# One hand-written instruction order for blocks 1 to 6 of the feed-forward half of an FNet layer

## The chip, the cores and the metric

The kernel runs on one core of a Trainium2 chip. Its engines are TensorE (PE, with its weight loads shown apart as PEld), VectorE (DVE), ScalarE (ACT), GpSimd (POOL) and SyncE (SP). The metric is device time in microseconds for one launch. Lower is better.

## The reference

The input x has 2048 rows of 576 values. It is normalised row by row, and three things are added: x itself, a Fourier mixing of the normalised rows, and a two-layer perceptron of them with 4608 hidden units.

```python
xn = layernorm(A_x)
a = xn @ dft_hid_re.T;  b = xn @ dft_hid_im.T
fourier = dft_seq_re @ a - dft_seq_im @ b          # 2048x2048 times 2048x576, twice
mlp = maximum(xn @ B_w1, 0) @ B_w2                 # 576 -> 4608 -> 576
out = A_x + fourier + mlp
```

## The kernel before

All products run in float16 as three partial products (high times high, high times low, low times high). So each operand is first scaled by a power of two and split: ACT writes the high half, DVE the remainder. Large products are done by seven block products in place of eight (Strassen's scheme), which adds sums and differences of operands on DVE.

The perceptron is cut into nine blocks of 512 hidden units (`b` = 0 to 8) and, inside each, four groups of 512 rows (`g` = 0 to 3). One `(b, g)` is a step, numbered t = 4b + g. A step has two pairs of hidden tiles (`i` = 0, 1). Each pair takes seven block products P1 to P7 of seven matmuls each (L495, function `product`), which gather in PSUM banks. What frees the banks is: a copy of P1, P6 and P5 on ACT (L521, L523, L524), and an addition of P2, P7 and P3 on DVE (L522, L525, L526). Then come the rectified values, split by ACT (L502) and DVE (L503), four sums on DVE (L506 to L509), and their split (L514 on ACT, L517 on DVE). The second layer of a step runs one step later: seven block products of twelve matmuls each (L566, `products2`; block 0 has four plain ones instead, L615), each followed by its eviction (L579 on ACT or L581 on DVE, `blocks2`). A finished sum is added to a buffer in DRAM by a DMA that POOL issues (L588, `add2`).

Beside this, each block prepares the weights of the next:

- SP loads two halves of w1, five DMAs each (L164, then L175 and L176 twice), and two of w2 (L152). All four halves share two buffers, `raw_w`.
- DVE takes the largest absolute value of each w1 half in two reductions (L652, `max_w1`). POOL finds it over the partitions (L202), and DVE makes the scale of it (L205 to L210, `power`). For w2, ACT sums absolute values (L718, `sum_w2`) and the same `power` follows.
- ACT and DVE split the weights (L676, L681, L682; L771, L775), and DVE forms the sums for Strassen's scheme (L698 to L701, L751 to L754).

Three more streams run along: SP loads tiles of the Fourier matrices (L1049, `first_c`), and ACT sums their absolute values (L1056, `sum_c`); there is one buffer for these tiles, so a load waits for the sum before it. In blocks 2 to 5 POOL issues one DMA in each step that adds a part of x to the DRAM buffer (L640, `add_x`).

Order is set in two ways. Between `begin()` and `end_hand()` every engine runs its instructions in the order in which the program writes them. Outside, a scheduler chooses each engine's order by its own estimates; `after(i)` holds an instruction behind another one there. Before the change, the hand order covers block 0 (a list of words, `ORDER`) and the first step of block 1, t = 4. The scheduler orders t = 5 to t = 35, where the loop over `steps` writes a step's products and takes pieces of weight preparation from the list `todo` at fixed points.

Of the kernel before, what the change touches and what calls it, by code (L numbers as in the profile page):

```python
# [18 lines left out]
P = 128  # L19
S = 2048  # L20
# [30 lines left out]
ORDER = """  # L51
# [24 lines left out]
tw:3:3 tu:3:2 od:3:3 tv:3:2:G rw:1 tw:3:2 rm:0  # L76
"""
# [3 lines left out]
def kernel(  # L81
# [394 lines left out]
    def pair_products(b, g, i):  # L476
# [5 lines left out]
        h = hs[b, g, i] = mlp.tile([P, 2, 7, GH], F16, tag="h", name=f"h{b}_{g}_{i}", bufs=4)  # L482
        st = mlp.tile([P, 5, GH], F32, tag="stage", name=f"s{b}_{g}_{i}")
        r21, s1, s2, s3, s4 = (st[:, n] for n in range(5))
        u, v, w = (banks1[k][0] for k in (i, 2, 3))
        c11, c22 = cbufs[i], cbufs[2]
        tt, stt = nc.vector.tensor_tensor, nc.vector.scalar_tensor_tensor

# [11 lines left out]
        def value(q, src):  # L500
            hi, lo = h[:, 0, q], h[:, 1, q]
            nc.scalar.activation(hi, src, AF.Relu)  # L502
            stt(lo, src, 0.0, hi, ALU.max, ALU.subtract)  # L503

        def end_s():
            stt(s3, c11, 0.0, r21, ALU.max, ALU.subtract)  # L506
            stt(s1, c22, 0.0, r21, ALU.max, ALU.add)
            stt(s2, c22, 0.0, s3, ALU.max, ALU.subtract)
            stt(s4, u, 0.0, s2, ALU.max, ALU.subtract)  # L509

        hi_s, lo_s = (h[:, k, S1 : S4 + 1] for k in range(2))

        def end_hi():
            order["s"] = nc.scalar.activation(hi_s, st[:, 1:], AF.Copy).ins  # L514

        def end_lo():
            order["lo"] = nc.vector.tensor_tensor(lo_s, st[:, 1:], hi_s, ALU.subtract).ins  # L517


        free = {  # L520
            P1: lambda: freed(nc.scalar.activation(c11, u, AF.Copy)),  # L521
            P2: lambda: freed(tt(c11, v, c11, ALU.add), "vfree"),  # L522
            P6: lambda: freed(nc.scalar.activation(s1, u, AF.Copy)),  # L523
            P5: lambda: freed(nc.scalar.activation(c22, w, AF.Copy)),  # L524
            P7: lambda: freed(tt(c22, u, c22, ALU.add), "vfree"),  # L525
            P3: lambda: freed(tt(r21, w, s1, ALU.add), "vfree"),  # L526
        }
        use = {
            P2: lambda: value(A11, c11),
            P7: lambda: value(A22, c22),  # L530
            P3: lambda: nc.scalar.activation(r21, r21, AF.Relu),
            P4: lambda: (value(A12, u), end_s(), ends.extend((end_hi, end_lo))),
        }

        def run(n, used=False):
            if used:
                return use[n]()
            product(n)
            if n in free:
                free[n]()  # L540
# [3 lines left out]
    places, sums = {}, {(r, j): None for r in range(2) for j in range(2)}  # L544
# [11 lines left out]
    def products2(b, g, n):  # L556

        qa, qb, first, row, col = PRODUCTS[n]
        if first:
            places[n] = ps2.tile([P, 2, 512], F32, tag="ps2", name=f"p2_{b}_{g}_{n}")[:, :, :EH]  # L560
        ps = places[PLACE[n]]
# [10 lines left out]
    def blocks2(b, g, n):  # L572

        row, col = PRODUCTS[n][3:]
        ps = places[PLACE[n]]
        o = sums[row, col]
        if n in (0, 2, 3, 6):
            o = sums[row, col] = sumbufs[sum_buffer(g, n)]
            freed(nc.scalar.activation(o, ps, AF.Copy, scale=us[b]))  # L579
# [4 lines left out]
    def add2(g, n):  # L584

        row, col = PRODUCTS[n][3:]
        if n not in (0, 2, 3):
            nc.gpsimd.dma_start(spill[g, row, col], sums[row, col], accum_op=ALU.add)  # L588
# [16 lines left out]
    def plain2(g, k):  # L605

        row, col = BLOCKS0[k]
        ps = places[0, k] = ps2.tile([P, 2, 512], F32, tag="ps2", name=f"p2_0_{g}_{k}")[:, :, :EH]
# [12 lines left out]
    def block2(g, k, eng=nc.scalar):  # L621

        o = sums[BLOCKS0[k]] = sumbufs[(4 * g + k) % 3]
        ps = places[0, k]
# [81 lines left out]
    def sum_w2(b, i):  # L706
# [3 lines left out]
        if b:  # L710
# [71 lines left out]
    def split_w2(b, i, c):  # L782
        if b and c == 0:
# [23 lines left out]
    def prepare_w2(b):  # L807
# [5 lines left out]
        if b == 1:  # L813
            p = steps1.pop(3)
# [676 lines left out]
```

## Time and profile before

| | |
|---|---|
| median of 3 runs | 1284.52 us (1283.21 to 1284.97) |
| the profiled execution, its own time | 1281.2 us |
| its span, first to last instruction | 1279.4 us |
| mean granted TensorE clock | 0.996 |
| PE busy in the span | 1222.7 us (96%) |
| DVE busy | 1019.5 us (80%) |
| ACT busy | 754.3 us (59%) |
| POOL busy | 213.9 us (17%) |
| DMA traffic | 175.97 MB, 138 GB/s on average |

Step t = 4 begins at 110.66 us in the span, block 2 at 204.11, block 7 at 638.94. Perceptron work ends near 812, and the two Fourier stages fill the rest. In the rows below, L-numbers are lines of the kernel before. `p` is a PSUM tile of the second layer, `bank` one of the first layer, `accs`, `dbuf` and `wbuf` are large SBUF buffers that hold several things. Where a row says "idle before", the engine sat idle ahead of that instruction, and the name behind the arrow is what ended the wait.

### The profile page before, as it was taken

How to read it: one execution, taken by the hardware profiler on the slowest of the kernel's cores; microseconds unless marked ns; L12 is line 12 of the kernel's file. 1: busy time of each engine (PE TensorE's matmuls, PEld its weight loads, DVE VectorE, ACT ScalarE, POOL GpSimd, SP SyncE). 2: the span in 40 equal slices, each digit the busy share in tenths (PEclk: the TensorE clock that was granted, in tenths of full speed). 3: DMA queues.
4: the chain of work that ended last, by engine and by line, in shares of the span. 5: the costliest groups of instructions: out<-in, count | busy, mean ns of one | idle time of the engine just before them, and what ended most of it. 6: DMA issues, size and time to landing. Idle time of an engine off the chain costs nothing.

```text
span 1279.4 us, 26160 instructions
## 1 busy us (share of the span) xinstructions
PE 1222.7 (96%) x10394; PEld 993.2 (78%) x10394; DVE 1019.5 (80%) x1968; ACT 754.3 (59%) x1334; POOL 213.9 (17%) x279
## 2 busy tenths in 40 slices
PE   6999999999998999999999999799999999999998
PEld 6856778788887887888888888576777777777777
DVE  7875887888877878988789878869877757888785
ACT  7664667667666676766776756645544445543332
POOL 2641111222132212111211111100111110000000
PEclk9999999999999999999999999989999999999999
DMA  7996565886778658666575777511755541155440
GB/s 225 201 190 163 130 133 117 172 170 114 166 147 168 130 121 177 141 142 145 122 156 119 161 168 162 135 36 66 199 116 144 116 101 24 59 190 161 154 127 33
DMA packets 127051, 175.97 MB, mean 138 GB/s; under 512 B 48336, under 2 KB 88784, under 8 KB 126928
## 3 DMA queue, kind: packets, MB, share of 16 engines
q1 hardware_dynamic: 98256, 122.38, 32.3%
q0 software_dynamic: 28672, 51.92, 27.4%
q8 instruction: 81, 1.33, 0.4%
q14 instruction: 42, 0.34, 0.1%
HBM read 112.53 MB, written 56.62 MB: 132 GB/s over the span
## 4 chain that ended last, share of the span: by engine, by line
PE 53%; DVE 19%; issue 12%; DMA 6%; ACT 5%; POOL 3%; SPq 1%; POOLq 0%; DVEq 0%; ACTq 0%
PE p L1358 20%; PE p L566 13%; PE bank L495 13%; PE pd L1211 6%; DMA raw_w<-in_w_dram 2%; POOL spill L588 2%; DVE h L517 1%; DVE cs L775 1%; DVE h L503 1%; DVE R L1171 1%; DVE w2s L775 1%; DMA accs<-in_x_dram 1%; DMA accs<-in_cim_dram 1%; DMA raw_d<-in_dft_dram 1%; ACT f L1056 1%
## 5 line engine op out<-in xcount | busy, mean ns | idle before, releaser
L566 PE MATMUL p<-w2s,h 128*128 128x288 f16 x2688 | 367.7, 286 | 9.8 <-ACT sums L579 2.5
L1358 PE MATMUL p<-R,cs 128*128 128x288 f16 x2688 | 333.4, 287 | 5.7 <-DVE accs L1368 3.4
L1358 PEld LDWEIGHTS <-cs 128*128 128x128 f16 x2688 | 263.3, 98 | 75.5 <-issue 5.1
L566 PEld LDWEIGHTS <-h 128*128 128x128 f16 x2688 | 262.2, 98 | 74.7 <-issue 10.1
L495 PEld LDWEIGHTS <-wbuf 128*128 128x128 f16 x1568 | 153.3, 98 | 31.5 <-issue 10.5
L495 PEld LDWEIGHTS <-dbuf 128*128 128x128 f16 x1568 | 153.1, 98 | 29.8 <-issue 8.6
L771 ACT ACTIVATE cs<-tb,sc_c 128x1024 f16<-128x1024 f32 x56 | 63.8, 1147 | 86.1 <-PE p L1358 50.6
L495 PE MATMUL bank<-xT,dbuf 128*128 128x256 f16 x896 | 111.6, 273 | 0.0
L495 PE MATMUL bank<-xT,wbuf 128*128 128x256 f16 x896 | 111.1, 273 | 0.3 <-ACT accs L524 0.3
L502 ACT ACTIVATE h<-accs 128x256 f16<-128x256 f32 x128 | 51.9, 412 | 90.3 <-DVE accs L525 67.5
L517 DVE TENSOR_TENSOR h<-s,h 128x1024 f16<-128x1024 f32 x64 | 78.0, 1219 | 22.9 <-ACT h L514 22.5
L588 POOL DMA_DIRECT2D spill<-dbuf x70 | 63.3, 923 | 190.7 <-DVE dbuf L581 165.4
L495 PE MATMUL bank<-accs,wbuf 128*128 128x256 f16 x672 | 86.4, 272 | 7.8 <-DVE accs L525 5.2
L775 DVE SCALAR_TENSOR_TENSOR cs<-tb,sc_c,cs 128x1024 f16<-128x1024 f32 x56 | 71.5, 1281 | 27.5 <-ACT cs L771 27.1
L495 PE MATMUL bank<-accs,dbuf 128*128 128x256 f16 x672 | 86.7, 272 | 6.0 <-DVE accs L525 3.4
L514 ACT ACTIVATE h<-s 128x1024 f16<-128x1024 f32 x64 | 67.5, 1055 | 25.5 <-DVE s L509 25.1
L771 ACT ACTIVATE cs<-accs,sc_c 128x1024 f16<-128x1024 f32 x39 | 44.2, 1145 | 56.8 <-PE p L1358 25.6
L588 POOL DMA_DIRECT2D spill<-wbuf x42 | 38.2, 910 | 190.7 <-DVE wbuf L581 172.7
L1056 ACT ACTIVATE f<-f 128x1024 f32<-128x1024 f32 x64 | 66.9, 1046 | 1.0 <-DMA f<-in_cim_dram 0.9
L503 DVE SCALAR_TENSOR_TENSOR h<-accs,h 128x256 f16<-128x256 f32 x128 | 52.8, 417 | 15.9 <-ACT h L502 15.3
L775 DVE SCALAR_TENSOR_TENSOR cs<-accs,sc_c,cs 128x1024 f16<-128x1024 f32 x39 | 50.0, 1281 | 16.2 <-ACT cs L771 15.8
L1178 ACT ACTIVATE R<-tb 128x288 f16<-128x288 f32 (+1 forms) x64 | 39.3, 621 | 37.8 <-DVE tb L1202 29.0
(226 smaller groups left out, 1877.1 us busy)
## 6 DMA issues: line engine op xcount, KB each, us to landing
spill<-dbuf POOLq DMA_DIRECT2D x80, 288.0 KB, 4.7
f<-in_cre_dram SPq DMA_DIRECT2D x32, 512.0 KB, 5.7
f<-in_cim_dram SPq DMA_DIRECT2D x32, 512.0 KB, 5.7
spill<-wbuf POOLq DMA_DIRECT2D x48, 288.0 KB, 5.0
raw_w<-in_w_dram SPq DMA_DIRECT2D x18, 576.0 KB, 4.4
raw_w<-in_w_dram SPq DMA_DIRECT2D x17, 512.0 KB, 6.7
accs<-in_cim_dram SPq DMA_DIRECT2D x16, 512.0 KB, 4.8
tb<-in_cre_dram SPq DMA_DIRECT2D x16, 512.0 KB, 4.8
```

The costliest lines, as they stand in the source:

```text
L495: nc.tensor.matmul(ps, l, r, start=first and m == 0, stop=m == len(todo) - 1, skip_group_check=not first,)
L502: nc.scalar.activation(hi, src, AF.Relu)
L503: stt(lo, src, 0.0, hi, ALU.max, ALU.subtract)
L514: order["s"] = nc.scalar.activation(hi_s, st[:, 1:], AF.Copy).ins
L517: order["lo"] = nc.vector.tensor_tensor(lo_s, st[:, 1:], hi_s, ALU.subtract).ins
L566: nc.tensor.matmul(ps[:, c], h[:, x, qa, c * P : (c + 1) * P], w[:, y, qb], start=first and i == 0 and j == 0, stop=i == NQ - 1 and j == 2 ...
L588: nc.gpsimd.dma_start(spill[g, row, col], sums[row, col], accum_op=ALU.add)
L771: nc.scalar.activation(hi, src, AF.Copy, scale=s)
L775: nc.vector.scalar_tensor_tensor(lo, src, s, hi, ALU.mult, ALU.subtract)
L1056: nc.scalar.activation(f, f, AF.Abs, scale=2.0**-10, accum_out=sums_c[:, n, q : q + 1])
L1211: nc.tensor.matmul(ps, x[:, k, c * P : (c + 1) * P], dsp[z][:, a, y], start=first and m == 0, stop=m == len(PASSES) - 1, skip_group_check= ...
L1358: nc.tensor.matmul(ps, w[:, a, RANK[k]], r[:, c, RIGHT[rq]], start=first and k == 0 and j == 0, stop=k == HK - 1 and j == 2, skip_group_ch ...
```

## The change

The hand order is extended to t = 27, the last step of block 6. `ORDER` becomes `BLOCK0`, unchanged, and three lists follow: `BLOCK1` (blocks 1 and 2), `BLOCK` (one block, run four times, for blocks 3 to 6) and `FLUSH` (three words left over). A word names one small piece of work and where it belongs: `p:0:1:5` is product P5 of pair 1 in the block's step 0; `f:` frees its bank (a trailing A or V names ACT or DVE); `h:` and `l:` are the split of rectified values, `r:`, `x:`, `y:`, `H:`, `L:` the rest of a pair's work. `m:-1:4` is the second layer's block product number 4 of the step before, `e:` its eviction, `a:` its addition in DRAM, `X:` the addition of x. `F:` and `S:` are `first_c` and `sum_c`. For the next block's weights, `L1:` and `L2:` load w1 and w2, `mx:` is a w1 reduction, `sw:` the sum of w2, `R:` starts `power` on POOL and `ph:` ends it on DVE, `nh:`, `nl:`, `uh:`, `ul:` are the splits and `ns:`, `us:` the sums. The scheduler now orders t = 28 to t = 35 alone.

```diff
-ORDER = """
+BLOCK0 = """
+BLOCK = """
+p:0:0:1 e:-1:0:A F:1:0 a:-2:6 p:0:0:5 ul:0:0:2 f:0:0:1:A X:1 m:-1:1 ul:0:1:1 f:0:0:5:A L1:1:0
+p:0:0:6 e:-1:1 S:1:0 m:-1:2 a:-1:1 f:0:0:6:A p:0:0:2 L1:1:1 e:-1:2:V m:-1:3 f:0:0:2 h:0:0:11
+l:0:0:11 m:-1:4 e:-1:3:V m:-1:5 F:1:1 e:-1:4 mx:1:0 a:-1:4 m:-1:6 e:-1:5 mx:1:1 a:-1:5 p:0:0:3
+e:-1:6:A R:1:0 p:0:0:7 f:0:0:3 a:-1:6 ph:1:0 r:0:0 p:0:1:5 f:0:0:7 nh:1:0:0 mx:1:2 p:0:1:1
...
+        def copy_of(dst, src, eng):
+            if eng is nc.scalar:
+                freed(nc.scalar.activation(dst, src, AF.Copy))
+            else:
+                freed(nc.vector.tensor_copy(dst, src), "vfree")
...
+        def free(n, eng=nc.scalar):
+            if n in (P1, P5):
+                copy_of(*{P1: (c11, u), P5: (c22, w)}[n], eng)
+            elif n == P6:
+                copy_of(stage_of(1), u, eng)
...
-    def blocks2(b, g, n):
+    def blocks2(b, g, n, eng=nc.scalar):
...
+            if eng is nc.scalar:
+                freed(nc.scalar.activation(o, ps, AF.Copy, scale=us[b]))
+            else:
+                freed(nc.vector.tensor_scalar(o, ps, us[b], None, ALU.mult), "vfree")
...
-    for n in range(4, len(steps)):
+    def run_block(words, b, stop):
+        for word in words.split():
+            name, at, *args = word.split(":")
+            at = int(at) + (b if name in by_block else b * NG)
+            key = (name, at, *(a for a in args if a not in ENG))
+            late = at > stop // NG if name in by_block else at >= stop - (name in "mea")
+            late = late or key in held
+            if key in done or late or name == "X" and not 2 * NG <= at < 6 * NG:
+                continue
+            done.add(key)
...
+    LAST = 7 * NG
+    held = {(c, LAST - 1, "1") for c in "HLS"}
+    run_block(BLOCK1, 1, LAST)
+    for b in range(3, NB - 2):
+        run_block(BLOCK, b, LAST)
+    run_block(FLUSH, NB - 3, LAST)
+    ends += [pair(LAST - 1, 1)["H"], pair(LAST - 1, 1)["L"]]
+    end_hand()
+    passes = passes[2 * (LAST - NG) :]
+    for n in range(LAST, len(steps)):
...
-        if n == NG:
-            end_hand()
```

The instructions are the same but for 24 evictions that move from ACT to DVE (12 copies of 256 columns, 12 scalings of 576); and the values that `sum_w2` throws away go to the w2 tile in place of a staging tile. Three places show what the lists do to the order.

First DVE, at the head of block 3, around the two reductions of the first w1 half of block 4 (`raw_w1_4_0`). `h3_1_0` is a value of block 3, group 1, pair 0; `p2_3_0_1` is the second layer's product 1 of block 3, group 0. Before:

```order
L581 SCALAR_TENSOR_TENSOR wbuf_97<-p2_3_0_1_4307,c_ub_4050,wbuf_97 128x576
L525 TENSOR_TENSOR accs_98<-bank0_1754,accs_98 128x256
L503 SCALAR_TENSOR_TENSOR h3_1_0_4240<-accs_98,h3_1_0_4240 128x256
L522 TENSOR_TENSOR accs_98<-bank2_1756,accs_98 128x256
L526 TENSOR_TENSOR s3_1_0_4241<-bank3_1757,s3_1_0_4241 128x256
L652 TENSOR_REDUCE c_mf_4414<-raw_w1_4_0_4295 128x1
L503 SCALAR_TENSOR_TENSOR h3_1_0_4240<-bank0_1754,h3_1_0_4240 128x256
L506 SCALAR_TENSOR_TENSOR s3_1_0_4241<-accs_98,s3_1_0_4241 128x256
```

And with the change (L805 is `max_w1` there, L732 and L734 are evictions in `blocks2`, L632 and L628 free banks):

```order
L628 TENSOR_TENSOR accs_98<-bank2_1756,accs_98 128x256
L619 SCALAR_TENSOR_TENSOR h3_0_0_4105<-accs_98,h3_0_0_4105 128x256
L732 TENSOR_SCALAR wbuf_97<-p2_2_3_3_4091,c_ub_2821 128x576
L734 SCALAR_TENSOR_TENSOR wbuf_97<-p2_2_3_0_3995,c_ub_2821,wbuf_97 128x576
L805 TENSOR_REDUCE c_mf_4139<-raw_w1_4_0_4047 128x1
L734 SCALAR_TENSOR_TENSOR dbuf_96<-p2_2_3_3_4091,c_ub_2821,dbuf_96 128x576
L805 TENSOR_REDUCE c_mf_4139<-raw_w1_4_0_4047 128x1
L814 TENSOR_REDUCE c_mw1_4136<-c_mf_4139 128x1
L632 TENSOR_TENSOR s3_0_0_4075<-bank3_1757,s3_0_0_4075 128x256
```

The reductions moved from the work of block 3's group 1 to that of its group 0, a step earlier, with one eviction between them and the freeing of a bank (L632) behind.

Second SP, the same load. `f4_1` and the like are tiles of the Fourier matrices. Before:

```order
L1049 DMA f4_0_4085<-in_cre_dram 128x1024
L164 DMA raw_w1_4_0_4295<-in_w1_dram 128x4x256
L1049 DMA f4_1_4209<-in_cim_dram 128x1024
L175 DMA raw_w1_4_0_4295<-in_w1_dram 96x2x128
L176 DMA raw_w1_4_0_4295<-in_w1_dram 32x2x128
L175 DMA raw_w1_4_0_4295<-in_w1_dram 96x2x128
```

And with the change:

```order
L1202 DMA f4_2_4019<-in_cim_dram 128x1024
L256 DMA raw_w1_4_0_4047<-in_w1_dram 128x4x256
L267 DMA raw_w1_4_0_4047<-in_w1_dram 96x2x128
L268 DMA raw_w1_4_0_4047<-in_w1_dram 32x2x128
L267 DMA raw_w1_4_0_4047<-in_w1_dram 96x2x128
```

A Fourier tile stood inside the load of a w1 half and now stands ahead of it; the next one follows both halves.

Third POOL, where the largest value of block 4's w2 is found over the partitions (`ISA top`). Before:

```order
L588 DMA spill2_10_111<-wbuf_97 128x576
L640 DMA spill2_01_110<-in_x_dram 256x1x288
L640 DMA spill2_10_111<-in_x_dram 256x1x288
L202 ISA top_5108<-c_mw2_4982 128x2
L588 DMA spill3_00_113<-dbuf_96 128x576
```

And with the change:

```order
L793 DMA spill1_11_108<-in_x_dram 256x1x288
L741 DMA spill1_00_105<-dbuf_96 128x576
L741 DMA spill1_11_108<-wbuf_97 128x576
L294 ISA top_4800<-c_mw2_4685 128x2
L741 DMA spill1_01_106<-dbuf_96 128x576
```

The search stood right behind two additions of x, the second to the DRAM tile that an addition from `wbuf` had just been sent to. Now two additions from SBUF stand between the last addition of x and the search.

More of the change, by code (lines that the diff above doesn't have):

```diff
@@ L528, in pair_products @@
[L528 to L540, printed above, removed]
+            hi, lo = high_low(SUMS)
+            order["lo"] = nc.vector.tensor_tensor(lo, stage_of(slice(1, 5)), hi, ALU.subtract).ins
@@ L1054, in sum_c @@
         f = firsts.pop(m)
-        with after(order.get("free", order["s"])):
+        with after(order.get("free", order.get("s"))):
             nc.scalar.activation(
@@ L1084 @@
             ]
-        if 2 <= b < 2 + NG:
-            add_x(n - 2 * NG)
-        first, second = (pair_products(b, g, i) for i in range(NQ))
+        first, second = (old_pair(n, i) for i in range(NQ))
         later1, later2 = (lambda q, f=f: f(q, True) for f in (first, second))
```

242 lines of the change are left out of this document (201 added, 41 removed).

## The prediction

> **What bounds the kernel now.** I read the page's busy shares first, then the stretches of the perceptron, then the waits of PE in them, then the timeline around the longest. The page says that PE is the engine to fill:
>
> ```profile
> PE 1222.7 (96%) x10394; PEld 993.2 (78%) x10394; DVE 1019.5 (80%) x1968; ACT 754.3 (59%) x1334; POOL 213.9 (17%) x279
> ```
>
> The next view has busy times by stretch (length, then PE, PEld, DVE, ACT, POOL, granted clock, DMA share, GB/s). First comes the part of block 0 that runs in hand order after its start-up, then step 4, the rest of block 1, blocks 2 to 6, one quiet step, and block 7.
>
> ```profile
> 30.00:110.66 80.66, 77.70 (x701) 55.62 (x698) 64.27 (x146) 51.79 (x95) 39.53 (x54) 1.00 0.96 190
> 110.66:137.01 26.35, 23.30 (x197) 18.96 (x196) 12.73 (x36) 14.05 (x29) 3.59 (x6) 1.00 0.43 115
> 137.01:204.11 67.10, 64.36 (x549) 53.14 (x547) 57.38 (x123) 42.28 (x84) 13.03 (x16) 1.00 0.65 143
> 204.11:292.21 88.10, 85.00 (x730) 71.19 (x728) 71.63 (x158) 59.19 (x117) 20.30 (x25) 1.00 0.75 150
> 292.21:377.93 85.72, 84.44 (x731) 71.20 (x729) 71.49 (x158) 58.98 (x115) 16.88 (x21) 1.00 0.71 147
> 377.93:466.64 88.71, 84.76 (x731) 71.21 (x729) 71.36 (x158) 58.92 (x115) 19.45 (x24) 1.00 0.71 146
> 466.64:553.51 86.87, 85.08 (x731) 71.04 (x729) 71.85 (x166) 59.70 (x117) 18.26 (x23) 1.00 0.70 145
> 553.51:638.94 85.43, 84.52 (x730) 71.15 (x728) 71.84 (x159) 59.00 (x115) 15.23 (x20) 1.00 0.66 140
> 575.83:596.82 20.99, 20.99 (x184) 17.81 (x182) 17.63 (x39) 13.62 (x28) 3.52 (x5) 1.00 0.56 122
> 638.94:723.98 85.04, 84.42 (x730) 71.14 (x728) 73.44 (x162) 59.64 (x117) 14.70 (x19) 1.00 0.63 138
> ```
>
> The quiet step is the floor: PE runs all its matmuls without a gap in 20.99 us, so a block costs at least 83.96. The excess over it is 4.14, 1.76, 4.75, 2.91 and 1.47 us in blocks 2 to 6, and 67.10 - 62.97 = 4.13 in the last three steps of block 1. For step 4 I need the unit times of the two kinds of product (start, duration, count):
>
> ```profile
> 586.36 0.93 PE L495 MATMUL bank<-accs,wbuf 128*128 128x256 f16 x7
> 587.12 1.63 PE L566 MATMUL p<-w2s,h 128*128 128x288 f16 x12
> 588.59 0.93 PE L495 MATMUL bank<-accs,wbuf 128*128 128x256 f16 x7
> ```
>
> From start to start, a first-layer product takes 0.76 us and a second-layer one 1.47. Step 4 holds 14 of the first and, in its four plain products, 8 times twelve matmuls of the second kind: 10.7 + 11.8 and 0.1 for two tiny ones, 22.6 us, so its excess is 3.75. Together 22.9 us can be won between 110.66 and 638.94. Nothing more: PE work is unchanged.
>
> What PE waits for there is DVE, through the banks that DVE frees, and DVE in its turn for two of the loads of w1 (who waits for whom; us in total, times, longest):
>
> ```profile
> PE bank L495 <- DVE accs L525: 6.7, 7, 2.0
> PE bank L495 <- ACT accs L521: 3.8, 4, 1.6
> DVE c_mf L652 <- DMA raw_w<-in_w_dram: 4.3, 2, 3.2
> ```
>
> DVE is busy for 71.5 us of a block's 84. It is late because it stands still at the wrong word. The longest such wait, by the timeline:
>
> ```profile
> 387.55 1.04 POOL L640 DMA_DIRECT2D spill<-in_x_dram  x1 [6.04 <-DMA spill<-wbuf]
> 388.15 0.79 POOL L202 PARTITION_ALL_REDUCE top<-c_mw  x1
> 388.98 0.17 DVE L205 TENSOR_SCALAR half<-top 128x2 f32<-128x2 f32 x1 [3.96 <-POOL top L202]
> 390.19 0.42 DVE L525 TENSOR_TENSOR accs<-bank,accs 128x256 f32<-128x256 f32 x1
> 390.66 0.92 PE L495 MATMUL bank<-accs,wbuf 128*128 128x256 f16 x7 [2.04 <-DVE accs L525]
> ```
>
> POOL waits 6.04 us for an addition to land before it can add x to the same tile. The search for the largest w2 is queued behind, DVE stands 3.96 us at `half`, the bank behind that is freed late, and PE loses 2.04. The second kind is the load of w1:
>
> ```profile
> 403.90 0.62 SPq L164 DMA_DIRECT2D raw_w<-in_w_dram  x1
> 414.66 0.95 DVE L652 TENSOR_REDUCE c_mf<-raw_w 128x1 f32<-128x768 f32 x1 [1.09 <-DMA raw_w<-in_w_dram]
> 488.62 0.61 SPq L164 DMA_DIRECT2D raw_w<-in_w_dram  x1
> 501.47 0.95 DVE L652 TENSOR_REDUCE c_mf<-raw_w 128x1 f32<-128x768 f32 x1 [3.17 <-DMA raw_w<-in_w_dram]
> 510.29 0.93 PE L495 MATMUL bank<-accs,dbuf 128*128 128x256 f16 x7 [1.38 <-DVE accs L525]
> ```
>
> In blocks 4 and 5 what the first reduction reads landed 10.8 and 12.9 us after the load's issue, DVE waited 1.09 and 3.17, and the second time PE lost 1.38 us later on.
>
> **The change part by part.** *The search for w2 leaves the tail of POOL's queue.* In the lists two additions from SBUF stand between the last addition of x and the search, and the search has a word of its own ahead of its use. The 2.04 us of block 4 should go, and what is late next is nothing: four DVE words lie between `R:1:2` and `ph:1:2`, and cover the search.
>
> *The lists as such.* I counted `BLOCK` through by hand with start-to-start durations. PE needs 84.0 us, and I found no place where a bank is freed after PE wants it, if data from DRAM is in time. The tightest place is the block's head, after m:-1:4 ends. These rows give the durations (mean ns after the count):
>
> ```profile
> L581 DVE SCALAR_TENSOR_TENSOR dbuf<-p,c_ub,dbuf 128x576 f32<-128x576 f32 x56 | 45.2, 810 | 7.9 <-PE p L566 7.8
> L652 DVE TENSOR_REDUCE c_mf<-raw_w 128x1 f32<-128x768 f32 x36 | 33.5, 942 | 6.4 <-DMA raw_w<-in_w_dram 6.4
> 562.92 1.22 DVE L517 TENSOR_TENSOR h<-s,h 128x1024 f16<-128x1024 f32 x1
> 564.05 0.45 DVE L754 TENSOR_TENSOR raw_w<-raw_w 128x288 f32<-128x288 f32 x1
> ```
>
> The last two show that a DVE instruction starts about 0.08 us before its predecessor's end. So DVE does e:-1:4, mx:1:0, e:-1:5, mx:1:1 and a small reduction in 0.05 + 0.73 + 0.86 + 0.73 + 0.86 + 0.08 = 3.3 us, then f:0:0:3 in 0.35. PE meanwhile runs m:-1:5, m:-1:6, p:0:0:3 and p:0:0:7, 4.47 us, and then p:0:1:5 wants the bank that f:0:0:3 frees. The reserve is 0.8 us.
>
> *The w1 load.* L1:1:0 is issued when ul:0:0:2 has let its buffer go. From its place in the list to mx:1:0, PE does two first-layer and three second-layer products, 5.9 us, and DVE one eviction: 6.7 us. DVE reaches ul:0:0:2 one word of 0.73 earlier at least, so 7.4. With the reserve PE feels a landing later than 8.2 us. Six loads (for blocks 2 to 7) are bounded so: if none is late, nothing; if two are as late as those above, (10.8 - 8.2) + (12.9 - 8.2) = 7.3 us. The order on SP speaks for the lower part, since no Fourier tile stands inside a load any more. Against it, the load for block 3, which `BLOCK1` holds, is closer to its reduction (L1:2:0 to mx:2:0: four first-layer products and one of the second, 4.5 us), so DVE will stand there; but the next word that PE wants, e:3:4, is due two second-layer products later. I take 3.5.
>
> Loads slow each other down, as the DMA view shows (issues, KB each, median us to landing; the first two rows from 484 to 502 us, the third from 229 to 236.5):
>
> ```profile
> spill<-in_x_dram POOLq DMA_DIRECT2D x3, 288.0 KB, 7.2
> raw_w<-in_w_dram SPq DMA_DIRECT2D x4, 32.0 KB, 9.2
> ...
> raw_w<-in_w_dram SPq DMA_DIRECT2D x4, 32.0 KB, 4.6
> ```
>
> With POOL's additions of x beside them the same pieces took 9.2 us, otherwise 4.6. The Trainium skill has the same (page "DMA: Bandwidth & Descriptors", section "Issuing engines are not separate DMA queues"): transfers of all issuing engines run on the same 16 DMA engines and interleave. By that rule moving words between SP and POOL would gain nothing while as many bytes are in flight, and the term would stay at 7.3; the trace agrees that loads slow down beside POOL's additions, but four of six were not crowded enough to stop DVE.
>
> *Evictions moved to DVE.* 12 copies and 12 scalings. The copy is not in the trace; its bounds are the same width on ACT (L524, 378 ns) and an addition from PSUM on DVE (L525):
>
> ```profile
> L525 DVE TENSOR_TENSOR accs<-bank,accs 128x256 f32<-128x256 f32 x64 | 26.6, 415 | 4.5 <-PE bank L495 4.3
> L524 ACT ACTIVATE accs<-bank 128x256 f32<-128x256 f32 x64 | 24.2, 378 | 9.4 <-PE bank L495 7.3 <-DVE s L508 1.0 <-PE p L566 0.8
> L628 DVE TENSOR_SCALAR dbuf<-p,c_ub 128x576 f32<-128x576 f32 x4 | 3.1, 783 | 0.0
> ```
>
> I take 0.42 and 0.78: 14.4 us more on DVE over seven blocks, 2.1 each. That makes 73.6 of 84, so PE hides it; without that cover it would cost up to 14.4.
>
> *Small waits.* An order of fixed words also meets late neighbours that my count can't see. The nearest row is the hand order of block 0: its stretch above loses 80.66 - 77.70 = 2.96 us, and the waits of PE there are
>
> ```profile
> PE p L615 <- ACT dbuf L626: 1.9, 1, 1.9
> PE p L390 <- DMA xT<-dbuf: 0.5, 2, 0.3
> PE p L236 <- DVE mb L728: 0.5, 1, 0.5
> ```
>
> The first happens once, at the start of the second layer. The rest is 1.0 us in 80.66, 1.2%. On the 505.4 us of floor (528.28 - 22.9) this is 6.3. The ends are 0 (the count closes) and 3.7%, 18.5.
>
> *Blocks 7 and 8* are still scheduled, but from another start. Block 7's excess is 1.08; it may move by a us either way; I take nothing.
>
> The sum: 22.9 - 3.5 - 6.3 = 13.1 us gained. The span goes from 1279.4 to 1266.3. The profiled execution's own time, 1281.2, is 1.8 more than its span and 3.3 less than the median of the runs, so the median becomes 1284.5 - 13.1 = 1271.4, say 1271.
>
> **The rivals.** *The lists run almost dry of waits* (no late load, small waits 1 to 5): a gain of 17 to 22, 1262 to 1267. For it: the count closes, and the quiet step sits at the floor already, with DVE busy for 17.6 us of 21.
>
> *The lists lose what the scheduler lost.* Small waits at block 0's full 3.7% and loads at 3.5 eat 22.0 of 22.9: 1283.6, no change. For it: that is the only hand order in the trace; against: its long wait is a one-off, and DMA there is at a share of 0.96, against 0.7 later. A page of the skill points here too ("VectorE: DVE Perf Modes", section "The DRAIN you can't avoid"): the next operation starts only once the pipe is empty. By that rule 160 DVE instructions of a block would take up to 160 x 0.08 = 12.8 us more than my 73.6, 86.4 for 84, and PE would lose 2.4 us in each of seven blocks, 16.8 in all, which with the two terms above is no gain. The rows at 562.92 and 564.05 contradict it.
>
> *Slower: the reductions of w1 stop DVE in every block.* The lists put mx 7.4 us behind the issue, where the trace had 10.8 and 12.9 in the late cases; and behind mx stand an eviction and the freeing of the bank that PE wants in 0.8 us, where the scheduler had looser words. If all six loads land like that at 488.62, PE loses 6 x (12.9 - 8.2) = 28.2, with 6.3 of small waits 34.5: 11.6 slower, 1296. It turns slower than can be told from no change when each load costs over (22.9 + 2.6 - 6.3)/6 = 3.2, a landing past 11.4 us. One of six did that.
>
> *The change does not do what it says*: the lists could leave the critical words where they were. The order speaks against it.
>
> **How the numbers follow.** 0.2% is 2.6 us, about what a measurement of this kernel can tell from no change. The forecast (a gain of 8 to 17) has 0.47; almost no waits 0.19; a small gain of 3 to 8, from loads at 7.3 and more small waits, 0.11; no change 0.09; slower 0.14. So faster 0.77, same 0.09, slower 0.14. The range 1262 to 1288 leaves out the better part of the slower case and the last of the gain.
>
> **What would show it.** In the profile after, the stretches of blocks 3 to 6 should take 84 to 86 us each, alike, with DVE near 73.6; the wait of `half` on POOL's `top` should be near 0; reductions of `raw_w` should show what DMA wait is left, and any PE wait should be on f:0:0:3's line right behind. If blocks 3 to 6 show the same wait of 3 us or more, the w1 term is wrong. If they sit at the floor and the total has not moved, blocks 1, 2, 7 or 8 took it.

## The result, and the profile after

The median with the change is 1273.66 us (1272.1 to 1276.66, 4 runs) against 1283.87 us before (1281.81 to 1284.97, 4 runs): a ratio of 0.9925, 95% interval 0.9902 to 0.9948. That is 10.2 us faster, where 13.1 was forecast; 1271 was predicted, with a range of 1262 to 1288. The profiled execution took 1273.5 us, its span 1271.7. The total came out close. The stretches in which the gain was expected did not.

First the page's busy times, then the view of busy times by stretch (length, then PE, PEld, DVE, ACT, POOL, granted clock, DMA share, GB/s): step 4, the rest of block 1, blocks 2 to 8.

```profile
PE 1221.7 (96%) x10394; PEld 996.1 (78%) x10394; DVE 1041.7 (82%) x1992; ACT 747.0 (59%) x1310; POOL 215.4 (17%) x279
```

```profile
110.86:134.96 24.10, 23.05 (x197) 19.07 (x196) 15.98 (x43) 14.50 (x28) 3.59 (x6) 1.00 0.59 174
134.96:199.31 64.35, 62.28 (x536) 52.19 (x534) 57.59 (x130) 41.66 (x81) 12.12 (x15) 1.00 0.68 153
199.31:287.68 88.37, 87.55 (x754) 73.57 (x752) 82.79 (x181) 65.64 (x126) 19.48 (x23) 1.00 0.76 151
287.68:373.63 85.95, 84.30 (x731) 71.24 (x729) 74.49 (x162) 57.64 (x112) 19.75 (x23) 1.00 0.74 151
373.63:462.60 88.97, 85.69 (x730) 71.80 (x728) 74.72 (x162) 57.54 (x112) 19.62 (x23) 0.98 0.72 147
462.60:550.84 88.24, 85.91 (x730) 72.07 (x728) 74.66 (x162) 57.87 (x112) 18.46 (x22) 0.98 0.70 143
550.84:633.46 82.62, 82.62 (x718) 70.03 (x716) 73.02 (x160) 53.49 (x104) 15.16 (x19) 1.00 0.60 124
633.46:719.50 86.04, 84.60 (x731) 71.20 (x728) 70.22 (x154) 57.71 (x112) 14.92 (x19) 1.00 0.64 131
719.50:803.73 84.23, 83.13 (x720) 70.16 (x718) 69.55 (x142) 54.23 (x111) 14.20 (x17) 1.00 0.73 167
```

Blocks 3 to 6 run the same list, and should have been alike. Block 6 has no gap on PE at all; blocks 3, 4 and 5 are longer, and in 4 and 5 the granted clock is 0.98. The lists move some second-layer products over the borders of blocks (718 to 754 matmuls in a stretch of one block), so a stretch's floor has to be counted: 14 x 0.765 us for each step and 1.47/12 = 0.1225 us for each second-layer matmul. The table gives what each kernel loses over it, in us, one profiled execution each. The second column is a second profile of the kernel before; the last four are experiments told below.

| | before | before, again | after | after without x | before without x | x late | all together |
|---|---|---|---|---|---|---|---|
| step 4 | 3.8 | 3.9 | 1.5 | 2.1 | 7.4 | 0.8 | 0.6 |
| rest of block 1 | 4.1 | 4.2 | 2.8 | 3.3 | 4.0 | 3.7 | 1.3 |
| block 2 | 4.1 | 4.1 | 1.4 | 1.2 | 1.6 | 2.5 | 3.0 |
| blocks 3 to 6 | 10.7 | 13.5 | 11.3 | 0.4 | 3.8 | 0.4 | 1.1 |
| block 7 | 1.0 | 1.0 | 2.0 | 2.1 | 1.1 | 2.1 | 0.4 |
| block 8 | 5.4 | 5.3 | 1.5 | 3.3 | 5.5 | 4.1 | 2.1 |

Blocks 3 to 6, most of the change, gained nothing against the first profile of before, and 2.2 us against the second. Their loss after it lies in the first steps of blocks 3, 4 and 5, with 2.0, 5.0 and 4.3 us (0.1 in block 6). The waits there, for blocks 3 to 6 (DVE) and 110 to 634 us (PE):

```profile
DVE c_mf L805 <- DMA raw_w<-in_w_dram: 8.3, 3, 3.4
...
DVE half L297 <- POOL top L294: 0.4, 2, 0.2
```

```profile
PE bank L606 <- DVE s L632: 4.2, 3, 2.3
PE bank L606 <- DVE accs L628: 2.3, 2, 1.6
PE bank L606 <- ACT accs L596: 1.0, 1, 1.0
```

DVE stands at a reduction of w1 (L805), once in each of three blocks. In blocks 3 and 5 it is the first reduction of the first half, and PE then wants the bank that DVE frees behind it (L632). The timeline of block 5 shows the chain: POOL's addition of x, the first piece of the load on SP's queue (L256), the two reductions, the freeing of the bank, PE.

```profile
464.06 1.41 POOL L793 DMA_DIRECT2D spill<-in_x_dram  x1
464.80 0.61 SPq L256 DMA_DIRECT2D raw_w<-in_w_dram  x1
...
475.38 0.95 DVE L805 TENSOR_REDUCE c_mf<-raw_w 128x1 f32<-128x768 f32 x1 [2.83 <-DMA raw_w<-in_w_dram]
476.98 0.94 DVE L805 TENSOR_REDUCE c_mf<-raw_w 128x1 f32<-128x768 f32 x1
478.03 0.41 DVE L632 TENSOR_TENSOR s<-bank,s 128x256 f32<-128x256 f32 x1
...
478.50 0.71 PE L606 MATMUL bank<-accs,dbuf 128*128 128x256 f16 x5 [2.33 <-DVE s L632]
```

The reduction starts 10.6 us after the load's issue, PE waits 2.33 us, and the step loses 4.3. The rest is the clock. Microsecond by microsecond, granted clock in the third column from the right:

```profile
476.00:477.00 1.00, 0.17 (x2) 0.00 (x0) 1.00 (x3) 0.00 (x0) 0.00 (x0) 1.00 1.12 265
477.00:478.00 1.00, 0.00 (x0) 0.00 (x0) 0.96 (x3) 0.00 (x0) 0.64 (x1) 1.00 1.06 288
478.00:479.00 1.00, 0.50 (x5) 0.45 (x5) 0.74 (x6) 0.42 (x1) 0.83 (x3) 1.00 0.87 221
479.00:480.00 1.00, 1.00 (x9) 0.82 (x8) 1.00 (x4) 0.96 (x2) 0.62 (x1) 0.78 0.94 170
480.00:481.00 1.00, 1.00 (x7) 0.72 (x5) 1.00 (x4) 1.00 (x3) 0.00 (x0) 0.50 1.14 204
481.00:482.00 1.00, 1.00 (x7) 0.69 (x6) 0.59 (x2) 0.42 (x2) 0.00 (x0) 0.50 1.03 145
482.00:483.00 1.00, 1.00 (x7) 0.71 (x6) 0.42 (x1) 0.81 (x2) 0.00 (x0) 0.52 0.79 145
```

After a gap of 2.33 us PE gets half its clock for 0.44 + 1 + 1 + 0.96 = 3.4 us, which costs 1.7. Block 4 has such a stretch too, but another chain in front of it:

```profile
387.23 0.42 DVE L630 TENSOR_TENSOR accs<-bank,accs 128x256 f32<-128x256 f32 x1
391.07 0.95 DVE L805 TENSOR_REDUCE c_mf<-raw_w 128x1 f32<-128x768 f32 x1 [3.41 <-DMA raw_w<-in_w_dram]
...
391.27 0.92 PE L606 MATMUL bank<-accs,wbuf 128*128 128x256 f16 x7 [1.02 <-ACT accs L596]
393.74 1.23 PE L606 MATMUL bank<-xT,wbuf 128*128 128x256 f16 x7 [1.55 <-DVE accs L628]
```

Here the two reductions of the first half, at 383.50 and 385.08, waited for nothing: POOL had to wait 2.41 us for an earlier addition to land, so the addition of x went out at 377.81, 2 us behind the first piece of the load. It was the second half, whose load began at 378.82, that came late. DVE stood at its first reduction until 391.07, 12.25 us after that, with the freeing of a bank (L628) a few words behind. ACT was late too, by another way: its eviction at 388.27 had waited 7.50 us for an addition from `dbuf` to land, and its copy (L596) that ended the first of the two gaps is five instructions behind.

### The profile page after: what moved, and what is told of

It is laid out like the page before. It is cut to its first block, busy times and chain, and to the rows that moved or that the text cites. A ratio compares the mean times of both kernels' runs of the same rounds, so it can differ in the third digit from the quotient of the medians.

```text
span 1271.7 us, 26114 instructions
## 1 busy us (share of the span) xinstructions
PE 1221.7 (96%) x10394; PEld 996.1 (78%) x10394; DVE 1041.7 (82%) x1992; ACT 747.0 (59%) x1310; POOL 215.4 (17%) x279
## 4 chain that ended last, share of the span: by engine, by line
PE 58%; DVE 17%; DMA 9%; issue 8%; ACT 5%; POOL 2%; SPq 1%; ACTq 0%; DVEq 0%; POOLq 0%
PE p L1578 21%; PE bank L606 15%; PE p L716 14%; PE pd L1431 6%; DMA raw_w<-in_w_dram 3%; PE p L768 1%; DMA accs<-in_x_dram 1%; DVE h L653 1%; DVE w2s L928 1%; DVE R L1391 1%; DVE cs L928 1%; DMA xT<-wbuf 1%; POOL spill L741 1%; DMA f<-in_cre_dram 1%; DVE tb L1406 1%
## 5 line engine op out<-in xcount | busy, mean ns | idle before, releaser
L716 PE MATMUL p<-w2s,h 128*128 128x288 f16 x2688 | 359.1, 286 | 4.8 <-DVE sums L734 2.3
L730 ACT ACTIVATE dbuf<-p,c_ub 128x576 f32<-128x576 f32 x64 | 47.1, 735 | 36.2 <-PE p L716 17.9
L596 ACT ACTIVATE accs<-bank 128x256 f32<-128x256 f32 x123 | 46.7, 379 | 36.3 <-PE bank L606 26.3
```

What stands on the lines that cost most here:

```text
L716: nc.tensor.matmul(ps[:, c], h[:, x, qa, c * P : (c + 1) * P], w[:, y, qb], start=first and i == 0 and j == 0, stop=i == NQ - 1 and j == 2 ...
```

## The experiments

In all of them the theory to test is that the additions of x, which POOL issues in blocks 2 to 5 and not in block 6, make the w1 loads land late. Times of "before" beside each run are those of its own chip.

**Without x.** After the change, and before it:

```diff
-            if key in done or late or name == "X" and not 2 * NG <= at < 6 * NG:
+            if key in done or late or name == "X":
```
```diff
-        if 2 <= b < 2 + NG:
-            add_x(n - 2 * NG)
```

> The changed kernel without the additions of x to the DRAM buffer in blocks 2 to 5 (x is then missing from the sum). In the changed kernel the first steps of blocks 3, 4, 5 and 6 take 21.5, 24.5, 23.8 and 19.6 us, and DVE stands 2.1, 3.4 and 2.8 us at a reduction of w1 in the first three; block 6 has no addition of x. Theory 1 (the additions of x, in flight with the w1 loads, make them land late): the three steps fall to 19.6 to 20.0 us, the waits at the reductions to under 0.5, the time by 10 to 11 us, to 1262 to 1264. Theory 2 (the w1 halves, the Fourier tiles and the sums fill the DMA engines by themselves, x is a tenth of it): the waits keep two thirds of their size, the time falls by 2 to 5, to 1269 to 1272.

> The kernel before without the additions of x (x is then missing from the sum). Its blocks 2 to 5 lose 13.6 us over the floor. Theory 1 (POOL's tail of additions in front of the w2 search and the late w1 loads are what the scheduled order loses most by, and both come from the additions of x): the excess of blocks 2 to 5 falls to 5 to 7 us, the time by 6 to 9, to 1275 to 1278; with hand order and without x the two kernels then still differ by 10 or more. Theory 2 (the scheduler's losses are in its order of words, whatever the transfers do): within 3 us of before, 1281 to 1285.

Measured: 1268.83 us (1264.7 to 1270.69) and 1273.04 (1271.81 to 1277.93), with 1282.42 before; ratios 0.9882 (0.9851 to 0.9913) and 0.9931 (0.9909 to 0.9954). Blocks 3 to 6 by stretch, of the kernel after and then of blocks 2 to 5 of the kernel before, both without x:

```profile
289.63:373.72 84.09, 84.09 (x731) 71.25 (x729) 74.57 (x162) 57.91 (x112) 15.18 (x19) 1.00 0.68 143
...
541.90:624.52 82.62, 82.62 (x718) 70.06 (x716) 72.97 (x160) 53.75 (x104) 15.18 (x19) 1.00 0.62 125
```

```profile
209.10:294.69 85.59, 84.67 (x731) 71.19 (x729) 71.63 (x158) 59.20 (x117) 15.02 (x20) 1.00 0.68 138
294.69:380.54 85.85, 84.43 (x731) 71.23 (x728) 71.50 (x158) 58.98 (x115) 14.94 (x20) 1.00 0.67 139
380.54:465.06 84.52, 84.28 (x731) 71.23 (x729) 71.35 (x158) 58.94 (x115) 14.99 (x20) 1.00 0.69 139
465.06:549.33 84.27, 84.11 (x731) 71.21 (x729) 72.26 (x166) 60.30 (x117) 15.41 (x21) 1.00 0.69 140
```

The list without x runs on the floor to 0.1 us. In the stretches theory 1 holds for both kernels: 10.9 us go in blocks 3 to 6 after the change, and before it blocks 2 to 5 fall from 13.4 to 4.2 (the median fell by 9.4, a little more than expected). The last clause of the second expectation fails. Without x the two kernels differ by 4.2 us and not by 10: a large part of what I had put down to the scheduler's order was what both orders lose by x. The changed kernel's time fell by less than its stretches: in the profiled execution block 8, the start and the stretch behind the perceptron took 1.9, 1.2 and 2.2 us back.

**x later.** The same addition, but behind the search of the second w1 half:

```diff
-f:0:0:1:A X:1 m:-1:1
+f:0:0:1:A m:-1:1
-R:1:1 l:0:1:11
+R:1:1 X:1 l:0:1:11
```

> The changed kernel with the first of a block's four additions of x moved in blocks 3 to 5 from the block's head, ahead of the w1 load, to behind the search of the second w1 half. Theory 1 (the addition of x slows the load): the pieces of w1 land 5 to 7 us after issue as in block 6, in place of 8 to 11, the first steps of blocks 3 to 5 fall to 19.6 to 20.5 us, the time by 8 to 11, to 1263 to 1266. Theory 2 (the load is slow by its own bytes and the sums' beside it): landings of 7 to 9, the steps fall by less than 1 us each, 1270 to 1274.

Measured: 1269.13 us (1268.63 to 1270.97), ratio 0.9893 (0.9872 to 0.9913). Two rows for the pieces of w1 in the DMA view (issues, KB each, median us to landing) of the 15 us at the head of block 5, with the change, and then with x late:

```profile
raw_w<-in_w_dram SPq DMA_DIRECT2D x2, 512.0 KB, 8.8
raw_w<-in_w_dram SPq DMA_DIRECT2D x4, 96.0 KB, 8.7
```

```profile
raw_w<-in_w_dram SPq DMA_DIRECT2D x2, 512.0 KB, 6.9
raw_w<-in_w_dram SPq DMA_DIRECT2D x4, 96.0 KB, 5.7
```

Blocks 3 to 5 by stretch, x late:

```profile
291.03:375.12 84.09, 84.09 (x731) 71.20 (x729) 74.56 (x162) 57.59 (x112) 19.61 (x23) 1.00 0.79 155
...
459.21:543.30 84.09, 84.09 (x730) 71.21 (x728) 74.65 (x162) 57.67 (x112) 18.43 (x22) 1.00 0.76 151
```

The landings come 2 to 3 us sooner, and blocks 3 to 5 sit on the floor as without x, with the same bytes in a block. So theory 1 is shown: it is what shares the DMA engines with the load in those 10 us that counts, not how much a block moves. The time was 3 us above its range: in the profiled execution the start took 2.2 us more than in the profile after, and blocks 2 and 8 lost 1.0 and 2.7 more.

**Reductions later.** The words of `BLOCK` from `F:1:1` to `R:1:1`, on one line each side where nothing changed is left out:

```diff
-e:-1:4 mx:1:0 a:-1:4 m:-1:6 e:-1:5 mx:1:1 a:-1:5 p:0:0:3 e:-1:6:A R:1:0 p:0:0:7 f:0:0:3
-a:-1:6 ph:1:0 r:0:0 p:0:1:5 f:0:0:7 nh:1:0:0 mx:1:2 p:0:1:1 h:0:0:22 x:0:0 p:0:1:2 nh:1:0:1
-f:0:1:1:A p:0:0:4 S:1:1 l:0:0:22 f:0:1:2 p:0:1:6 y:0:0 h:0:0:12 nl:1:0:1 f:0:1:5:A
+e:-1:4 a:-1:4 m:-1:6 e:-1:5 a:-1:5 p:0:0:3 e:-1:6:A p:0:0:7 f:0:0:3
+a:-1:6 r:0:0 p:0:1:5 f:0:0:7 mx:1:0 mx:1:1 R:1:0 p:0:1:1 p:0:1:2 f:0:1:2 h:0:0:22 x:0:0
+f:0:1:1:A ph:1:0 p:0:0:4 S:1:1 l:0:0:22 p:0:1:6 y:0:0 nh:1:0:0 h:0:0:12 nh:1:0:1 f:0:1:5:A
...
-p:0:1:7 mx:1:3 H:0:0 p:0:1:3 f:0:1:7 R:1:1
+p:0:1:7 nl:1:0:1 H:0:0 p:0:1:3 f:0:1:7 mx:1:2 mx:1:3 R:1:1
```

The second run moves one word of these again:

```diff
-ph:1:0 p:0:0:4 S:1:1 l:0:0:22
+ph:1:0 p:0:0:4 l:0:0:22
-f:0:1:6:A l:0:0:12 h:0:1:11 p:0:1:7
+f:0:1:6:A l:0:0:12 h:0:1:11 S:1:1 p:0:1:7
```

> The changed kernel with the reductions of w1 in blocks 3 to 6 put behind the freeing of the banks of P3, P7 and (second pair) P2, some 4.6 us of PE work later; loads and additions stay where they are. Theory 1 (PE loses only because the reduction stands in DVE's queue ahead of the bank that PE wants): the loads land as late as before, DVE may still stand at a reduction for up to 1 us, and PE's loss in the first steps of blocks 3, 4 and 5 falls from 2.0, 5.0 and 4.3 us to under 0.7 each; the time falls by 8 to 11, to 1263 to 1266. Theory 2 (the reductions and the split are late for what follows in any case): the loss moves to the second step of the block, 1270 to 1275.

> The kernel with late reductions (1295 us), with the sum of the Fourier tile S:1:1 moved on ACT from ahead of the two splits of w1 and the copies of P5 and P6 (second pair) to behind them. Theory 1 (what cost 22 us there was ACT standing 4.9 us at that sum, for a tile that SP loads behind both w1 halves; in the changed kernel DVE's wait at the reduction had covered it): the first steps of blocks 3 and 5 fall from 8.8 and 7.9 us over the floor to 1 to 4, the time to 1272 to 1283. Theory 2 (the eviction that waits 6.6 us for the addition of its buffer, or the reductions themselves, cost it): 1288 to 1297.

Measured: 1295.29 us (1293.27 to 1299.26), ratio 1.0098 (1.0071 to 1.0124); then 1283.93 (1281.05 to 1286.69), ratio 1.0007 (0.9992 to 1.0023). Both expectations of the first run are wrong; it is slower than either allowed. DVE indeed waited only 0.29 us at block 3's reduction. But the timelines of ACT and PE show who stood next:

```profile
303.08 0.74 ACT L730 ACTIVATE dbuf<-p,c_ub 128x576 f32<-128x576 f32 x1 [6.59 <-DMA spill<-dbuf]
...
311.35 1.06 ACT L1209 ACTIVATE f<-f 128x1024 f32<-128x1024 f32 x1 [4.93 <-DMA f<-in_cre_dram]
```

```profile
314.70 3.15 PE L606 MATMUL bank<-xT,dbuf 128*128 128x256 f16 x14 [6.54 <-ACT s L596]
```

The Fourier tile is loaded by SP behind both halves of w1 and lands with them; ACT stood 4.93 us at its sum, with the copy that PE wanted queued behind, and PE lost 6.54. With the reductions in their old place DVE's wait had delayed PE and, it seems, covered this one. Taking that word out of the way gives 11.4 us back: the first steps of blocks 3 and 5 fall from 8.8 and 7.9 us to 2.3 and 1.9. Of this 6.8 us are clock: in the first run 6.8 us ran at 0.50 in each of these two blocks, in the second none. That is theory 1 of the second run, whose time is 1 us above its range. What stays, 3.7 to 4.1 us in each of the four blocks, block 6 too, comes from my moved words and has nothing to do with x: PE waits 6.5 us for `s` of L632 and 5.8 for ACT's copy L596, in four blocks together.

**Fewer blocks by hand.** The lists order blocks 1 and 2 only. The scheduled loop of the changed kernel has no call of `add_x`, so the first of these runs left out twelve of the sixteen additions of x, which its expectation does not reckon with; the second has the call (last lines).

```diff
-    LAST = 7 * NG
+    LAST = 3 * NG
-    for b in range(3, NB - 2):
+    for b in range(3, 3):
-    run_block(FLUSH, NB - 3, LAST)
+    run_block(FLUSH, 2, LAST)
...
+        if n < 6 * NG:
+            add_x(n - 2 * NG)
```

> The changed kernel with the hand order ended after block 2: the lists order blocks 1 and 2 alone, the scheduler blocks 3 to 8 as before. In the profiled executions blocks 1 and 2 lost 12.0 us over the floor before and 5.8 with the change, blocks 3 to 6 10.7 before and 11.3 with the change, block 8 5.4 and 1.5. Theory 1 (the change gains in blocks 1 and 2 and at the end of block 8; the list repeated in blocks 3 to 6 gains nothing net, since late w1 loads cost it what it saves): blocks 1 and 2 lose 5 to 7, blocks 3 to 6 8 to 13 as before, and the time is 1274 to 1279, within 3 us of the whole change. Theory 2 (the repeated list carries half of the gain or more): 1279 to 1283.

> The hand order ended after block 2 again, now with an addition of x at the head of every scheduled step of blocks 3 to 5, as the kernel before has it. The run before this one had left those twelve additions out; its blocks 3 to 6 lost 4.9 us over the floor and its time was 1272.1. Theory 1 (with the additions the scheduled blocks 3 to 6 lose what they lost in the kernel before, 8 to 13 us, so the repeated list gains nothing net there): 1275 to 1280. Theory 2 (from its new start the scheduler finds a better order in blocks 3 to 6, additions or not): they lose under 6, 1271 to 1274, and the repeated list then costs more than it brings.

Measured: 1272.12 us (1268.38 to 1273.83), ratio 0.9905 (0.9877 to 0.9934), with most additions of x left out; then 1275.58 (1272.36 to 1280.18), ratio 0.9940 (0.9920 to 0.9959). With all additions, blocks 3 to 6 lost 9.0 us, inside theory 1's range, and the time is 1.9 above that of the whole change. So three quarters of the gain, 7.6 of 10.2 us, are there without the repeated list. Its intervals and the change's overlap, so I can't say that the list brings anything while x stays where it is.

**Evictions back to ACT**, from the kernel with x late: all fifteen `:V` of `BLOCK1` and `BLOCK` as in

```diff
-e:-1:2:V m:-1:3 f:0:0:2
+e:-1:2:A m:-1:3 f:0:0:2
```

> The kernel with the late addition of x (1269 us, blocks 3 to 6 on the floor), with all 24 evictions of the lists that are on DVE put back on ACT. Theory 1 (the move to DVE was free and is not what gains: ACT has room too, busy for 54 to 58 us of 84): blocks 3 to 6 stay within 0.5 us of the floor each, blocks 1 and 2 within 1.5 of 6.9, the time within 2, 1267 to 1271. Theory 2 (the moved evictions are the lists' way past ACT's queue, and banks would be freed late without them): 0.5 to 1.5 us lost at each, 1275 to 1290.

Measured: 1267.59 us (1266.64 to 1276.35), ratio 0.9900 (0.9867 to 0.9933), within theory 1: blocks 3 to 6 at 0.1 each over the floor, blocks 1 and 2 at 7.6. In blocks 3 to 6 the move of the evictions was not needed. In block 1 that is not shown. Two of the five runs took 1273.9 and 1276.4 us, and in the first of them, the profiled one, step 7 (the last of block 1) lost 3.4 us, against 0.0 to 1.3 in the other runs with `BLOCK1`:

```profile
198.27 1.16 ACT L871 ACTIVATE w2s<-raw_w 128x1152 f16<-128x1152 f32 x1 [3.69 <-DMA raw_w<-in_w_dram]
199.84 0.92 PE L606 MATMUL bank<-accs,dbuf 128*128 128x256 f16 x7 [3.24 <-ACT accs L596]
```

ACT stood at the sum of a late half of w2, and two copies that `BLOCK1` has on DVE (`f:3:1:1:V` and `f:3:1:5:V`) were queued behind. That is theory 2, in one place.

**An early search.** From the kernel with x late, one search of a tile of zeros more, as a word `W` behind `a:-1:3` of `BLOCK1`:

```diff
+            nc.gpsimd.memset(w[:, :1], 0.0)
+            nc.gpsimd.partition_all_reduce(w[:, 1:], w[:, :1], P, ReduceOp.max)
```

> The kernel with the late addition of x and one search over the partitions more, of a tile of zeros, on POOL right behind the last store of block 0. In all traces the first such search starts 3.9 to 8.5 us after its input is ready, later ones 0.1 to 0.2, and DVE and then PE wait for it in the third step of block 1, which loses 2.3 to 2.8 us. The program has an instruction without tile ahead of the first search. Theory 1 (that one takes POOL some 8 us once, and it now runs in a pause of POOL): the first search of w1 starts 0.2 us after its input, step 6 loses 0.5 to 1.2, the time is 1 to 2 shorter, 1267 to 1268. Theory 2 (the delay is of another kind, such as the input or a transfer): no change in step 6, 1268 to 1270.

Measured: 1265.59 us (1265.02 to 1266.31), ratio 0.9864 (0.9845 to 0.9884). POOL's first search in the profile after, and then the extra search and the first real one of this run:

```profile
142.50 0.92 POOL L741 DMA_DIRECT2D spill<-wbuf  x1 [9.33 <-DVE wbuf L734]
152.10 0.38 POOL L294 PARTITION_ALL_REDUCE top<-c_mw  x1 [8.68 <-issue]
```

```profile
134.48 0.12 POOL L1258 MEMSET warm<- 128x1 f32 x1
141.92 1.20 POOL L1259 PARTITION_ALL_REDUCE warm<-warm  x1 [7.33 <-issue]
143.93 1.05 POOL L741 DMA_DIRECT2D spill<-wbuf  x1 [0.80 <-DVE wbuf L734]
149.71 0.43 POOL L294 PARTITION_ALL_REDUCE top<-c_mw  x1 [4.73 <-DVE c_mw L814]
```

The gap in front of the first search moves to the extra one, where nobody waits for POOL, and step 6 falls from 2.75 us over the floor (x late) to 0.0. So theory 1 holds: the gap goes with the first search, wherever that stands. Between the medians lie 3.5 us, more than its 1 to 2, but they are of two chips, and the intervals of the ratios overlap.

**Block 7 by hand**, from the kernel with x late, one more turn of the list:

```diff
-    LAST = 7 * NG
+    LAST = 8 * NG
-    for b in range(3, NB - 2):
+    for b in range(3, 8):
-    run_block(FLUSH, NB - 3, LAST)
+    run_block(FLUSH, 7, LAST)
```

> The kernel with the late addition of x, with the repeated list run for block 7 as well; the scheduler orders block 8 alone. Theory 1 (what blocks 7 and 8 lose, 2.1 and 4.1 us, is the scheduler's, and the list removes the first): block 7 falls to under 0.3 us over the floor, the time to 1266 to 1268. Theory 2 (the scheduled block pays for the hand order that ends before it, and the loss moves on to block 8): 1268 to 1272.

Measured: 1265.90 us (1262.32 to 1267.76), ratio 0.9863 (0.9838 to 0.9888). Block 7 falls from 2.1 us over the floor to 0.1, as theory 1 has it, and block 8 from 4.1 to 2.4.

**All together** (x late, the early search, block 7 by hand, and block 2's addition of x moved in the same way), and the kernel before once more:

```diff
-p:4:1:5 X:5 F:5:0
+p:4:1:5 F:5:0
-e:4:0:A R:2:1 p:5:1:7
+e:4:0:A R:2:1 X:5 p:5:1:7
```

> The changed kernel with all that helped: the first addition of x of a block behind the search of the second w1 half (in block 2 too), the extra early search on POOL, and the repeated list run for block 7. Theory 1 (the gains are of different stretches and add up): block 1 loses under 1.5 us, block 2 under 1.5, blocks 3 to 7 0.1 each, block 8 2 to 4; the time is 1260 to 1263. Theory 2 (the addition moved in block 2 only moves the jam there, and blocks 7 and 8 give back): 1264 to 1267.

> The kernel before once more, for a second profile of it. Theory 1 (the first profiled execution, 1281.2 us, was a fast one, and the missing 2.7 us to the median of all runs are lost in the stretches where transfers are waited for, block 0, step 4 and blocks 2 to 5): 1282 to 1286, block 0 or step 4 longer by 1 to 4 us, block 8 at 5 us over the floor again. Theory 2 (the difference lies behind the perceptron, in the Fourier stages): block 0 and blocks 1 to 8 within 1 us of the first profile.

Measured: 1262.91 us (1259.68 to 1264.39), ratio 0.9839 (0.9811 to 0.9867): 20.3 us less than before, twice the change. Block 1 lost 1.9 us and block 2 3.0, neither under 1.5, so moving block 2's addition of x did nothing that this profile shows. The kernel before took 1286.09 us in its second profile. These are its blocks 4 and 5:

```profile
378.57:469.10 90.53, 86.27 (x730) 71.98 (x728) 71.36 (x158) 58.72 (x115) 19.41 (x24) 0.98 0.71 143
469.10:556.97 87.87, 85.23 (x731) 71.02 (x729) 71.88 (x166) 59.57 (x117) 18.24 (x23) 1.00 0.72 143
```

They are 1.8 and 1.0 us longer than in the first. The start is later by 0.55 and the stretch behind the perceptron longer by 1.5, so both theories have a part of the 4.9 us between the spans. Block 8 is the same to 0.1.

## Why the prediction was right, and where it was not

*The total* was right by 2.7 us, but not by its terms, and that was luck. Between 110.66 and 638.94 us of the first profile 13.1 us were to be won; 528.28 became 522.60, so 5.7 were (8.6 by the second profile of before). Block 7 lost 1.0, block 8 gained 3.9, and the start and what comes behind lost 0.9: 7.7 from span to span. The remaining 2.5 of the 10.2 are the draw of the profiled execution: the first profile of before was a quick one.

*The w1 term is the step that failed.* I took 3.5 us, with 7.3 as the upper bound; it was 1.9 + 4.9 + 4.2 = 11.0. The mechanism was right, a load of w1 that stops DVE in front of a bank. The place (PE waits on L632, f:0:0:3's line) and the threshold were right for the first half of w1, in blocks 3 and 5. A landing later than 8.2 us after issue was to be felt: in blocks 3 and 5 the first reduction's last piece landed 9.7 and 10.5 us after the load's issue and PE waited 1.60 and 2.33, which puts the threshold at 8.1; in block 6 it landed after 7.3 us and cost nothing. Three things were missed. The term looked at the first half alone; in block 4, which lost most, the first half landed 6.0 us after issue, and the second half, for whose reduction I had worked out no reserve, stopped DVE. I counted two late loads because two were late before; but the lists put the load in every block beside the addition of x and the sums, and three of the four with x beside them made PE wait (in block 2 DVE stood 0.6 and 1.0 us, and PE was not held up at the bank). And in blocks 4 and 5 the gaps then cost 1.7 us of clock each, which I had not priced at all. PE's gaps in the three heads are 1.6 + 3.3 + 2.3 = 7.2, by chance the bound of 7.3, which was for two loads; the clock lies past it. The "slower" rival had its mechanism right, in three blocks of six: six like block 4, 4.9 us each, would have cost about the 28 us that it named.

*The argument for the low value was the wrong one*: no Fourier tile stands inside a load any more. The neighbour that mattered was on POOL's queue. The row for it stood in the prediction, 9.2 us against 4.6 with additions of x beside the load, and I used it to average, not to ask which of the two cases the lists make. The Trainium skill (page "DMA: Bandwidth & Descriptors", section "Issuing engines are not separate DMA queues") spoke against the change in the right place: transfers of all issuing engines share the same DMA engines. I had set it at 7.3. The trace agrees with its first half. What I drew from it, that moving words brings nothing while as many bytes are in flight, is contradicted by x late.

*The search for w2* went as forecast: DVE waits 0.4 us in all at `half` in blocks 3 to 6.

*Small waits*: 6.3 were forecast, and blocks 1 to 6 lost 17.0 - 11.0 = 6.0 besides the w1 term. But they were not spread evenly as a share of time. Blocks 3 to 6 have 0.1 each, so the hand count of `BLOCK` closed; 5.8 lie in blocks 1 and 2, with 2.3 in step 6, behind POOL's first search.

*Evictions on DVE* were hidden, as said. The copy took 401 to 425 ns (0.42 taken), the scaling 816 (0.78 taken); DVE is busy 74.5 to 74.7 us in blocks 3 to 5, 1 more than forecast. The rival in which each DVE instruction costs 0.08 us more is out: by it DVE would have had 86.4 us of work in a block, and with x late a block takes 84.09.

*Blocks 7 and 8* were put at nothing, within 1. Block 7 lost 1.0, as allowed. Block 8 gained 3.9, because its last step fell from 4.9 us over the floor (both profiles of before) to 0.4; 0.2 to 0.4 in every kernel with a longer hand order. In the other kernels of the table other steps of block 8 took up to 3 us of that back, so its worth there is 1 to 4; in two profiles (blocks 1 and 2 alone by hand, most of x left out; the second run with late reductions) they took more than all of it. Why the scheduler's last step differs was not tried, so the cause of these 3.9 us, over a third of the gain, stays open.

## What to carry over

Before a fixed order is blamed or praised, ask of each load in it what else is in flight in the ten microseconds before its first use, on all queues: here one DMA of 288 KB in each of three blocks, moved by 65 words or some 18 us, took 10.9 us of loss out of blocks 3 to 6, where the list as it stood had gained 2.2 at most. Where a late transfer stops one engine, look which other words wait for transfers of the same burst, since taking the first waiter away uncovers the next. A term bounded by the cases seen in the old trace is bounded only if the change does not make that case more frequent; and one profile of each kernel leaves some 3 to 5 us here to the draw.

## What was not expected of the hardware

- PE's clock. In block 5, after 2.33 us without a matmul, the granted clock fell to 0.50, about 1 us after PE had work again, and for 3.4 us. The length of the gap does not decide this: one of 2.05 us had such a tail (before without x, ended at 120.25), and one of 3.24 (evictions back to ACT, ended at 199.84) and one of 2.04 (before, ended at 390.66) had none. In each trace the stretches at 0.50 in the perceptron all begin on one raster of 3.41 us and last one or more of its cells. What goes with them is how much of the cell ahead PE was busy (length, then PE; the cell of the gap of 2.05, and the emptier of the two over which the 3.24 are spread):

```profile
118.35:121.76 3.41, 1.51 (x13) 1.13 (x13) 0.60 (x2) 2.55 (x5) 0.56 (x1) 1.00 0.86 154
197.84:201.25 3.41, 1.41 (x13) 1.27 (x13) 0.98 (x7) 2.98 (x7) 1.25 (x2) 1.00 0.64 99
```

  From 30 to 815 us of all the traces, each cell at full clock with PE busy for up to 0.40 of it was followed by 0.50 (0.32 in block 5), none above 0.45 was, and between the two, as in these rows (0.44 and 0.41), it came out either way. By this a gap of 2 to 3 us cost 1.7 us more where it fell into one cell, and nothing where a border of the raster split it. The Trainium skill (page "TensorE: Matmul & The Clock Gate", section "HAM oscillation — how this bites in real kernels") warns of gaps over some 3.4 us; the traces have the tail after shorter gaps.
- POOL's first search. In the traces of before, after, x late and the early search POOL stood 7.3 to 9.3 us ahead of it with nothing in the profile to wait for; later searches that waited for their input came 0.1 to 0.2 us after it. The Trainium skill (page "GPSIMD Engine Reference", section "2.1 Instruction dispatch") puts some 6 us on the first call of a freshly loaded kernel; the traces agree in kind and show 1 to 3 us more.
